# Reordering the expert block of a fused attention, expert and mixing kernel: first products evacuated and next tokens turned ahead of the split of the next expert's first weights

## The chip, the cores and the metric

One core of a Trainium2 chip runs the whole program. The metric is the device time of one execution in microseconds (us), the median of several executions; lower is better. Engines are named as in the profile: PE (matrix products and transposes), PEld (its weight loads), DVE (VectorE), ACT (ScalarE), POOL (GpSimd), SP (which issues most DMAs).

## What is computed

The reference is windowed attention over 4 batches of 576 tokens, then a layer of 8 experts that picks one expert for each token, then a gated mixing over the sequence. The change lies in the middle layer:

```python
for s in range(S):
    fresh_e = int(np.argmax(logits[b, s]))
    if s == 0 or local_gate[b, s] < 0.5:
        e = fresh_e
    else:
        e = prev_e if prev_e >= 0 else fresh_e
    prev_e = e
    ...
    h = np.maximum(x[b, s] @ w1[e], 0.0)
    out[b, s] = p[e] * (h @ w2[e])
```

A token has 512 values, an expert has w1 (512 x 1024) and w2 (1024 x 512), all float32.

## The kernel before

**Blocks.** Tokens are sorted into blocks of 128 rows that share an expert. At most 25 blocks exist; 23 (0 to 22) hold tokens in these runs, and the last ones stand inside branches. Which tokens a block has, which expert, and whether the expert differs from that of the block before, is computed on the chip (the routing) in three lists: blocks 0 and 1, blocks 2 to 5, blocks 6 to 24. The routing of the last batch still runs during blocks 0 to 2: its steps wait in a list `stages`, and `pop` puts some of them between the products (after the second quarter of stage 1 and after parts 2 and 6 of stage 2).

**Precision.** A float32 factor is used as the sum of a high part (a rounded copy, made by ACT) and a low part (the difference, by DVE or POOL). A product is then three matmuls: high x high (L999), low weights x high tokens (L1000), high weights x low tokens (L1001).

**One block.** `block(j)` (L1157) does stage 1 of block j+1 (`stage1`, 24 matmuls in four quarters kk, into the PSUM tile `hp`) and stage 2 of block j (`stage2`, 24 matmuls L1033 to L1035 in eight parts f, into `yp`), and around them:

- `gather` (L967): DVE copies an index column (L970), POOL issues the indirect DMA (L972) that brings the rows of a block into `xs`. It is called at the block's start for block j+3; the later calls with j+3 find it done.
- `fetch` (L564): SP issues four DMAs for a block's w1 into `raw1` or w2 into `raw2`, which move data only if the expert changes. Each has to wait until the pieces of the raw tile have been read.
- `divide` (L950): the split of the next weights, inside a branch (L958) that is taken if the expert changes. Four pieces c: ACT copies raw to the high part (L549), then DVE (c = 0, 2, 3) or POOL (c = 1) subtracts (L550). `divide(1, j+2)` makes `w1h` and `w1l`, `divide(2, j+1)` makes `w2h` and `w2l`. It is taken ten times for each. A piece of `w1h` can be overwritten once the quarter of stage 1 that reads it is done.
- `bend` (L1003): ACT takes the ReLU of the two halves of `hp` to `h` (L1006). It needs the end of stage 1.
- `turn_x` (L974): PE transposes the gathered rows of block j+2 to `xTp` (L976), ACT copies the high part `xh` (L984), DVE subtracts the low part `xl` (L985).
- `turn_h` (L1009): PE transposes `h` (L1012); in two halves ACT copies `hh` (L1022) and DVE subtracts `hl` (L1023), the second `hh` after the first `hl`. Stage 2 of the next block reads them.
- `narrow` (L1055): a piece of the mixing's float64 weights is turned to float32, in blocks 5 to 16: five DVE operations and one on ACT (L1065 to L1071), split one block later on ACT and POOL (tiles `wih`, `wil`, `woh`, `wol`).
- `place` (L478), the last routing step, comes in block 2 after part 2 of stage 2: DVE copies `bc` (L482), POOL multiplies (L486), DVE reduces and combines (L487 to L496).

**Order.** The order on each engine is the order of the calls, written by hand (`manual_schedule`); an engine runs its instructions in that order, and a waiting instruction holds those behind it. In `block(j)` it is, with the values that matter here: stage 1 of j+1, split of w1 for j+2, ReLU of j+1, turning of the tokens of j+2, stage 2 of j, split of w2 for j+1, store of j, turning of h of j+1.

Of the kernel before, what the change touches and what calls it, by code (L numbers as in the profile page):

```python
# [69 lines left out]
def moe_stack(ctx: ExitStack, tc: tile.TileContext, q, k, v, w_gate, w_local, w1, w2, w_in, w_sp, b_sp, w_out, out):  # L70
# [9 lines left out]

    # ---------------------------------------------------------------- constants
    warm = const.tile([128, 512], BF16, name="warm")
# [38 lines left out]

    # ---------------------------------------------------------------- routing state
    idxacc = rt.tile([128, NCOL], F32, name="idxacc")
    slot_i = rt.tile([128, LB], I32, name="slot_i")
    sel_all = rt.tile([128, LB, E], F32, name="sel_all")
    # of each token: its block among its expert's blocks, its row in it, and its weight
    trips = rt.tile([128, LB, 3], F32, name="trips")
# [7 lines left out]
    def steps(f):  # L135
        """A closure's parts, between which other work may come."""
        g = f()
        if g is not None:
            yield from g
# [9 lines left out]
    def router(b, xT, pieces, sides, bank):  # L149
        """Adds the closures that route batch b to stages."""  # L150
        st = {}
# [93 lines left out]
        def scan3():  # L245
            sv = st["sv"]
            if b == 0:
                # How many blocks of each expert hold tokens of the first batch.
                ci = rt2.tile([E, 2], I32, name="ci")
                nc.vector.tensor_scalar(out=ci[:, 0:1], in0=state["cum"], scalar1=127.0, scalar2=None, op0=ALU.add)  # L250
                nc.vector.tensor_scalar(out=ci[:, 1:2], in0=ci[:, 0:1], scalar1=7, scalar2=None, op0=ALU.arith_shift_right)
                state["first"] = rt.tile([E, 1], F32, name="first")
                nc.vector.tensor_copy(state["first"], ci[:, 1:2])
            nc.scalar.activation(sv[:, S:640], sv[:, 512:S].bitcast(F32), AF.Copy)
# [134 lines left out]
        def rows():  # L389
# [18 lines left out]
            if b < 3:  # L408
                return
            # The block before which every row of the first batch is there, if there is such a one.  # L410
            it = iota128[0:1, 0:n]
# [17 lines left out]
        def after():  # L429
            """Where this list's blocks of each expert begin, how many they are, and where the next list begins."""  # L430
            sf, en, nb, (j0, j1) = st["sf"], st["en"], st["nb"], LISTS[b]
            D = state["D"]
            base = rt2.tile([E, 1], F32, name="base")
            if b == 1:
                nc.vector.tensor_copy(base, sf)
            else:
                nc.vector.tensor_scalar(out=base, in0=sf, scalar1=state["got"], scalar2=float(j0), op0=ALU.subtract, op1=ALU.add)
            nc.vector.tensor_scalar(out=D[:, 2 * b - 2], in0=ident[0:E, 0:E], scalar1=base, scalar2=None, op0=ALU.mult)
            yield
            if b == 3:  # L440
                return
            n = j1 - j0
            tk = rt2.tile([E, 1], F32, name="tk")
            nc.vector.tensor_scalar(out=tk, in0=sf, scalar1=-1.0, scalar2=float(n), op0=ALU.mult, op1=ALU.add)
            yield
            nc.vector.tensor_scalar(out=tk, in0=tk, scalar1=0.0, scalar2=nb, op0=ALU.max, op1=ALU.min)
            yield
            got = rt.tile([E, 1], F32, name=f"got{b}")
            if b == 1:
                nc.vector.tensor_copy(got, tk)  # L450
            else:
                nc.vector.tensor_add(got, state["got"], tk)
            nc.vector.tensor_scalar(out=D[:, 2 * b - 1], in0=ident[0:E, 0:E], scalar1=got, scalar2=None, op0=ALU.mult)
            yield
            last = rt2.tile([E, 1], F32, name="last")
            nc.vector.tensor_scalar(out=last, in0=sf, scalar1=float(n), scalar2=None, op0=ALU.is_lt)
            yield
            l2 = rt2.tile([E, 1], F32, name="l2")
            nc.vector.tensor_scalar(out=l2, in0=en, scalar1=float(n), scalar2=None, op0=ALU.is_ge)
            yield  # L460
            nc.vector.tensor_mul(last, last, l2)
            yield
            st["last"], st["new"] = last, got
# [75 lines left out]
    stages = []  # L539
    state["bank"] = R()  # L540

    # ---------------------------------------------------------------- attention
    sc = ctx.enter_context(tc.tile_pool(name="sc", bufs=1))
# [11 lines left out]
    def fetch1(j, i):  # L555
        """The first two blocks have their own copies of w1, the first one also of w2, and use them as they are."""
        e = value(1, j, [ET.SP], E - 1)
        nc.sync.dma_start(first1[j][:, i:i + 1], w1[ds(e, 1), 128 * i:128 * i + 128].rearrange("o (k p) f -> p (o k) f", p=128))
# [23 lines left out]
    def attention(aw, ap, qkp, plan):  # L582
# [13 lines left out]
        npair = B * 4  # L596
        # A head's keys fill half of the rows and meet zeros in the other half, which lets the products use both heads' queries as they lie.
        kz = [[aw.tile([128, S], F32, name=f"kz{p}{hh}", bufs=1) for hh in range(2)] for p in range(2)]
# [4 lines left out]
        def load_qk(u):  # L603
            b, pr = divmod(u, 4)
            n, c = (96, 6) if pr < 2 else (72, 8)
            for w_, src in ((0, q), (1, k)):
                t = qkp.tile([96, 1024], F32, name=f"qk{w_}", bufs=3)
                if w_:
                    # Keys come head by head, each partition's tokens in one piece.
                    tv = t[0:n, 0:2 * c * D].rearrange("p (h m) -> p h m", h=2)  # L610
# [52 lines left out]
        def T_k(u, hh, tag="T"):  # L663
            """Turns a head's keys two neighbours at a time, whose dimensions then lie in the two halves of the rows."""
            def f():
# [157 lines left out]
        fill = deque()  # L823
# [14 lines left out]
        def feed(i):  # L838
            """Parts of the routing, as many as a step can take along; the tensor engine gets one only when its operands had time to be made."""
            nonlocal budget  # L840
# [83 lines left out]

    # ---------------------------------------------------------------- experts
    aps, aws, qks, w1s, mws, mps, xps = [ExitStack() for _ in range(7)]
# [34 lines left out]
    def own(key, pool, shape, dt, tag=None):  # L961
        """A tile that stays for all blocks."""
        if key not in P:
# [91 lines left out]
    def narrow(c):  # L1055
        """A piece of the float64 weights as float32, and that in two parts."""
        if c < 8:
# [16 lines left out]
    def early(kind, c=0):  # L1074
        """The steps of blocks 0 and 1 that run beside the last of the attention."""
        def bankT():
# [22 lines left out]
    def pop(kind="any"):  # L1099
        """The next step of the routing; "pe": if the tensor engine has a part in it; "rest": all up to such a one."""  # L1100
        while stages and (kind == "any" or (kind == "pe") == hasattr(stages[0], "on_pe")):
# [4 lines left out]
    def ahead(what, j, must=False):  # L1106
        """Issues the gathers or fetches up to block j that the lists already give."""
        while done[what] <= min(j, NBLK - 1):
# [35 lines left out]
    def gate(j, engines=None):  # L1144
        """Blocks that every count of tokens fills run straight, the others where they hold any."""
        if j < SURE:
# [10 lines left out]
    def block(j):  # L1157
# [4 lines left out]
        if nxt:  # L1162
            with gate(j + 1, [ET.PE]):
                for kk in range(4):
                    stage1(j + 1, hp, [kk])
                    if kk in POP1:
                        pop("pe")
                        pop("rest")
        if nxt2:
            ahead(1, j + 2, must=True)  # L1170
            divide(1, j + 2, j == 0)
        if nxt:
            bend(j + 1, hp)
        ahead(1, j + 3)
        if nxt2:
            ahead("gather", j + 2, must=True)
            turn_x(j + 2, bank_x())
        ahead("gather", j + 3)
        yp = bank_y()
        for f in range(8):  # L1180
# [46 lines left out]

    # ---------------------------------------------------------------- gated mixing over the sequence
    gr = ctx.enter_context(tc.tile_pool(name="gr", bufs=1, side="right", reuse_waits="tile"))
# [11 lines left out]
    def mixing(gw):  # L1241
# [17 lines left out]
        def turn_w(si):  # L1259
            """A part of the weights over the sequence, turned; the last 64 columns twice, for the two places of a batch's last tokens."""  # L1260
            w2x = G["w2x"]
# [61 lines left out]
        def norm3(g):  # L1323
            vr, _ = vn[g]
            if g % 9 == 4:
                # The last 64 tokens of two batches: a batch's high parts and, in the other half, its low parts.
                for t, a, z in ((tails[0], slice(0, 64), slice(64, 128)), (tails[1], slice(64, 128), slice(0, 64))):
# [59 lines left out]
        def project(b, gh, gl):  # L1387
# [3 lines left out]
            for ah, al, i in items:  # L1391
                o = gw.tile([128, C], F32, name="o", bufs=2)
                # The very last piece in two halves, so that less of it is left at the end.
                for cs in [slice(0, C)] if (b, i) != (B - 1, 3) else [slice(0, 256), slice(256, C)]:
# [86 lines left out]
```

## Time and profile before

| | us |
|---|---|
| median of 3 runs | 706.55 |
| lowest and highest run | 706.11, 706.99 |
| span of the profiled execution, first to last instruction | 705.2 |
| median run less that span (before the first and after the last instruction) | 1.35 |
| PE busy in the span | 672.2 (95%) |
| DVE, ACT, POOL busy | 423.9, 386.0, 194.2 |

The page gives no time of its own for the profiled execution beside its span, so the span and the 1.35 us around it are set against the median. The clock that the throttle granted PE is at 90% or more of full speed in all 40 slices. In rows of a timeline the columns are: start and duration in us, engine, source line, operation, output and inputs, count, and in brackets the idle time of the engine just before and what ended it. A merged row (x3) runs from the first start to the last end. A line with "DVEq" or "ACTq" names that engine's instruction sequencer, here at the branch of `divide`.

### The profile page before, as it was taken

Reading aid. Unit: us, or ns where it says so; the run is one execution under the profiler, and the core shown is the slowest. Engines: PE = TensorE matmul, PEld = TensorE weight load, DVE = VectorE, ACT = ScalarE, POOL = GpSimd, SP = SyncE. Lnnn points to the kernel's source line nnn. Section 1 sums busy time; section 2 is a strip of 40 time slices with the busy share of each in tenths; the row PEclk is TensorE's granted clock in tenths of the full one; section 3 lists DMA queues with packets and bytes.
Section 4 is the critical chain, followed back from the end, with each engine's and each line's share of the span. In section 5 each row is a group of like instructions: output and inputs, shape, how many; then the busy total and the mean of one; then the engine's idle time right before and its main releaser. Section 6 shows DMA issues by size and latency. Waiting matters only on the chain. (4 is left out here: it accounts for less than half of the span.)

```text
span 705.2 us, 14287 instructions
## 1 busy us (share of the span) xinstructions
PE 672.2 (95%) x4395; PEld 571.1 (81%) x4396; DVE 423.9 (60%) x1379; ACT 386.0 (55%) x780; POOL 194.2 (28%) x226
## 2 busy tenths in 40 slices
PE   8999898989999999999999999897999999999998
PEld 6989797885478788787788877775898998998997
DVE  4667869777966747877866656342664164154151
ACT  5788777653635646666665556333735336335322
POOL 6443434341424405425424254112010110000000
PEclk9999999999999999999999999999999999999999
DMA  6776545594446776586556746415110220200102
GB/s 152 180 174 152 129 118 131 189 347 126 138 150 204 249 283 231 199 314 213 192 195 223 283 142 233 165 32 162 30 46 0 76 60 1 75 16 1 60 2 74
DMA packets 90644, 101.36 MB, mean 144 GB/s; under 512 B 49984, under 2 KB 60992, under 8 KB 90560
## 3 DMA queue, kind: packets, MB, share of 16 engines
q1 hardware_dynamic: 87120, 89.10, 39.7%
q0 software_dynamic: 3440, 11.27, 5.0%
q8 instruction: 36, 0.59, 0.3%
q14 instruction: 48, 0.39, 0.2%
HBM read 139.68 MB, written 17.30 MB: 223 GB/s over the span
## 5 line engine op out<-in xcount | busy, mean ns | idle before, releaser
L1001 PE MATMUL hp<-w1h,xl 128*128 128x512 f32 x168 | 66.9, 398 | 7.0 <-DVEq L958 6.1
L1033 PE MATMUL yp<-w2h,hh 128*128 128x512 f32 x176 | 71.6, 407 | 0.2 <-ACT hh L1022 0.2
L1035 PE MATMUL yp<-w2h,hl 128*128 128x512 f32 x176 | 69.9, 397 | 1.7 <-DVE hl L1023 1.7
L972 POOL DMA_INDIRECT xs<-x_d,ix x25 | 30.8, 1232 | 144.7 <-PE xTp L976 56.1
L1034 PE MATMUL yp<-w2l,hh 128*128 128x512 f32 x176 | 69.6, 395 | 0.0
L743 POOL TENSOR_TENSOR ms<-ms,mxa 96x384 f32<-96x384 f32 (+2 forms) x64 | 51.1, 799 | 64.9 <-DVE mxa L740 39.7
L999 PE MATMUL hp<-w1h,xh 128*128 128x512 f32 x168 | 68.4, 407 | 0.2 <-issue 0.2
L1000 PE MATMUL hp<-w1l,xh 128*128 128x512 f32 x168 | 66.4, 395 | 0.0
L740 DVE CUSTOM_DVE_ANT_0 ms<-S,masks 96x128 f32<-96x128 f32 (+2 forms) x224 | 54.4, 249 | 16.8 <-PE S L729 8.2
L550 DVE TENSOR_TENSOR w2l<-raw,w2h 128x1024 fp32r<-128x1024 f32 x30 | 48.7, 1649 | 24.5 <-ACT w2h L549 24.2
L550 DVE TENSOR_TENSOR w1l<-raw,w1h 128x1024 fp32r<-128x1024 f32 x30 | 55.7, 1902 | 5.3 <-ACT w1h L549 4.6
L729 PE MATMUL S<-kz,qT 128*96 128x128 f32 (+2 forms) x448 | 53.2, 259 | 0.4 <-POOL vt L632 0.4
L1151 POOL DMA_INDIRECT yg<-y_d,slot_i x14 | 13.4, 958 | 138.5 <-PE tr L1283 102.6
L776 PE MATMUL PV<-vt,ptS 128*96 128x65 f32 (+2 forms) x448 | 44.4, 240 | 7.0 <-issue 2.9
L1023 DVE TENSOR_TENSOR hl<-hTp,hh 128x512 fp32r<-128x512 f32 x44 | 30.3, 689 | 33.9 <-ACT hh L1022 31.9
L1022 ACT ACTIVATE hh<-hTp 128x512 fp32r<-128x512 f32 x44 | 26.2, 596 | 43.6 <-DVE hl L1023 38.2
L776 PEld LDWEIGHTS PV<-vt,ptS 128*96 128x96 f32 (+2 forms) x448 | 38.7, 156 | 9.7 <-issue 3.6
L729 PEld LDWEIGHTS S<-kz,qT 128*72 128x72 f32 (+1 forms) x448 | 45.4, 155 | 1.2 <-POOL vt L626 0.9
L1001 PEld LDWEIGHTS hp<-w1h,xl 128*128 128x128 f32 x168 | 31.5, 188 | 17.1 <-DVEq L958 8.4
L549 ACT ACTIVATE w2h<-raw 128x1024 fp32r<-128x1024 f32 x40 | 41.1, 1060 | 6.0 <-PE yp L1035 3.4
L549 ACT ACTIVATE gtiles<-gt 128x288 fp32r<-128x288 f32 (+2 forms) x48 | 15.7, 359 | 48.0 <-DVE gt L1377 48.0
L1035 PEld LDWEIGHTS yp<-w2h,hl 128*128 128x128 f32 x176 | 33.1, 188 | 10.7 <-DVE hl L1023 3.0
(309 smaller groups left out, 1825.5 us busy)
## 6 DMA issues: line engine op xcount, KB each, us to landing
raw<-in_moe_w SPq DMA_DIRECT2D x188, 512.0 KB
y_d<-y SPq DMA_DIRECT2D x30, 256.0 KB
qk<-in_q SPq DMA_DIRECT2D x32, 144.0 KB
qk<-in_k SPq DMA_DIRECT2D x32, 144.0 KB
x_d<-xo SPq DMA_DIRECT2D x32, 144.0 KB
scratch<-in_moe_w_in SPq DMA_DIRECT2D x8, 512.0 KB
out<-o SPq DMA_DIRECT2D x15, 256.0 KB
vt<-in_v SPq DMA_DIRECT2D x48, 64.0 KB
```

Source lines behind the costliest of these rows:

```text
L549: nc.scalar.activation(dst_h, src, AF.Copy)
L550: (eng or nc.vector).tensor_tensor(out=dst_l, in0=src, in1=dst_h.bitcast(F32), op=ALU.subtract)
L729: nc.tensor.matmul(ps[0:nq, j, 0:nk], l, r, start=True, stop=True)
L740: nc.vector.tensor_tensor_reduce(out=ms[0:nq, j, 0:nk], in0=ps[0:nq, j, 0:nk], in1=masks[0:nq, m, 0:nk], scale=-0.125, scalar=3.0e38, op0= ...
L743: nc.gpsimd.tensor_tensor(out=ms[0:nq, 0:nb, 0:nk], in0=ms[0:nq, 0:nb, 0:nk], in1=mx[0:nq, 0:nb].unsqueeze(2).to_broadcast([nq, nb, nk]), ...
L776: nc.tensor.matmul(ops[0:nq, j], ptS[0:nk, j, 0:nq], r, start=True, stop=True)
L999: nc.tensor.matmul(ps[n], xh[:, kk], wh[:, kk, cs], start=(kk == 0), stop=False)
L1000: nc.tensor.matmul(ps[n], xh[:, kk], wl[:, kk, cs], start=False, stop=False)
L1001: nc.tensor.matmul(ps[n], xl[:, kk], wh[:, kk, cs], start=False, stop=(kk == 3))
L1033: nc.tensor.matmul(ps, hh[:, f], P["w2h"][:, f], start=(f == 0), stop=False)
L1034: nc.tensor.matmul(ps, hh[:, f], P["w2l"][:, f], start=False, stop=False)
L1035: nc.tensor.matmul(ps, hl[:, f], P["w2h"][:, f], start=False, stop=(f == 7))
```

## The change

The split of the next w1 and the fetch behind it move from between stage 1 and the ReLU to behind the turning of the next tokens. Nothing else differs but comments, which are gone.

```diff
@@ def block(j)
-        if nxt2:
-            ahead(1, j + 2, must=True)
-            divide(1, j + 2, j == 0)
         if nxt:
             bend(j + 1, hp)
-        ahead(1, j + 3)
         if nxt2:
             ahead("gather", j + 2, must=True)
             turn_x(j + 2, bank_x())
         ahead("gather", j + 3)
+        if nxt2:
+            ahead(1, j + 2, must=True)
+            divide(1, j + 2, j == 0)
+        ahead(1, j + 3)
         yp = bank_y()
```

## Rows read from the trace of the kernel before

**Rows 1.** Stretches of one block: length, PE, PEld, DVE, ACT, POOL, clock, DMA, GB/s.
```profile
309.90:322.40 12.50, 12.50 (x62) 10.21 (x61) 11.27 (x13) 9.27 (x14) 4.59 (x4) 1.00 0.64 237
296.10:309.90 13.80, 12.80 (x62) 10.18 (x61) 8.89 (x13) 7.65 (x12) 6.59 (x5) 1.00 0.70 243
440.30:455.20 14.90, 12.74 (x59) 10.12 (x60) 5.06 (x7) 3.43 (x7) 0.97 (x2) 1.00 0.49 177
232.40:246.00 13.60, 12.70 (x62) 10.09 (x61) 9.99 (x10) 8.11 (x12) 5.78 (x3) 1.00 0.63 215
```

**Rows 2.** Waits of PE in the expert blocks: total, times, longest.
```profile
PE hp L1001 <- DVEq L958: 6.1, 5, 2.2
```

**Rows 3.** Timeline, block 12 and the start of block 13: w1 split taken.
```profile
341.79 3.91 ACT L549 ACTIVATE w1h<-raw 128x1024 fp32r<-128x1024 f32 x4
341.91 0.60 PE L976 MATMUL xTp<-ident,xs 128*128 128x128 f32 x4
344.06 5.71 DVE L550 TENSOR_TENSOR w1l<-raw,w1h 128x1024 fp32r<-128x1024 f32 x3 [0.42 <-ACT w1h L549]
344.38 1.74 POOL L972 DMA_INDIRECT xs<-x_d,ix  x1 [7.88 <-PE yp L1035]
345.60 1.06 ACT L1006 ACTIVATE h<-hp 128x512 f32<-128x512 f32 x2
346.34 3.43 DVE L550 TENSOR_TENSOR w1l<-raw,w1h 128x1024 fp32r<-128x1024 f32 x1
349.05 0.40 PE L1000 MATMUL hp<-w1l,xh 128*128 128x512 f32 x1
349.70 0.68 DVE L985 TENSOR_TENSOR xl<-xTp,xh 128x512 fp32r<-128x512 f32 x1
```

**Rows 4.** Timeline, block 11, where the w1 split is not taken.
```profile
329.39 0.60 PE L976 MATMUL xTp<-ident,xs 128*128 128x128 f32 x4
329.65 1.09 ACT L1006 ACTIVATE h<-hp 128x512 f32<-128x512 f32 x2 [2.26 <-PE hp L1001]
330.62 0.60 ACT L984 ACTIVATE xh<-xTp 128x512 fp32r<-128x512 f32 x1
331.26 0.69 DVE L985 TENSOR_TENSOR xl<-xTp,xh 128x512 fp32r<-128x512 f32 x1 [2.01 <-ACT xh L984]
331.82 1.30 POOL L550 TENSOR_TENSOR wil<-scratch,wih 128x512 fp32r<-128x512 f32 x1 [0.87 <-ACT wih L549]
```

**Rows 5.** Timeline, block 2 and the start of block 3.
```profile
212.18 2.40 POOL L550 TENSOR_TENSOR w1l<-raw,w1h 128x1024 fp32r<-128x1024 f32 x1
212.52 4.28 DVE L550 TENSOR_TENSOR w1l<-raw,w1h 128x1024 fp32r<-128x1024 f32 x2 [0.51 <-ACT w1h L549]
212.57 0.60 PE L976 MATMUL xTp<-ident,xs 128*128 128x128 f32 x4
217.32 0.18 DVE L482 COPY bc<-R 128x40 f32<-128x40 f32 x1
223.94 0.69 DVE L1023 TENSOR_TENSOR hl<-hTp,hh 128x512 fp32r<-128x512 f32 x1 [0.94 <-DVEq L958]
226.30 0.40 PE L1034 MATMUL yp<-w2l,hh 128*128 128x512 f32 x1
226.53 0.40 PE L1035 MATMUL yp<-w2h,hl 128*128 128x512 f32 x1
```

**Rows 6.** Timeline, end of block 3 and block 4: both splits follow each other.
```profile
232.74 2.93 POOL L550 TENSOR_TENSOR w2l<-raw,w2h 128x1024 fp32r<-128x1024 f32 x1 [1.55 <-ACT w2h L549]
233.95 5.08 DVE L550 TENSOR_TENSOR w2l<-raw,w2h 128x1024 fp32r<-128x1024 f32 x3
240.21 0.40 PE L1035 MATMUL yp<-w2h,hl 128*128 128x512 f32 x1
```

**Rows 7.** Timeline, blocks 0 and 1: the list work on DVE and the product behind it.
```profile
194.41 0.17 DVE L386 TENSOR_TENSOR lz<-la,lz 8x19 f32<-8x19 f32 x1
195.18 0.35 PE L394 MATMUL R<-lz,onesE 8*1 8x19 f32 x8
```

## The prediction

> **What bounds the kernel now.** The summary of engines comes first: PE is busy in nearly all of the span, so only the gaps of PE can be won. The table of stretches shows where they are in the expert blocks: a clean block takes 12.50 us, all of it PE busy, and some blocks take more [rows 1]. The list of PE's waits names the place: five times PE stood before L1001, the product with the low part of the tokens, 6.1 us in all, released by DVE behind the branch of the split [rows 2]. The timeline of such a place gives the reason. In block 12 the three DVE pieces of the w1 split run from 344.06 to 349.77, and only then comes `xl`, which is short; `xl` ends at 350.38, while stage 1 of block 14 is under way and wants it 0.23 us after 349.05 [rows 3]. So the split of weights that are wanted later holds up tokens that are wanted first. ACT has the same order: `h` starts at 345.60, behind the four copies [rows 3], where without a split it starts 0.26 us after the first transpose [rows 4].
>
> A wait costs more than its idle time, since PE's pipeline fills again. The stretch 296.10 to 309.90 takes 13.80 us, 1.3 more than a clean block; there are four of that kind (13.8, 13.8, 13.7, 13.7), together 5.0 us. The stretch after block 19 takes 14.9, 2.4 more; the one at 232.40, 13.6, 1.1 more [rows 1].
>
> **The change, part by part.** Nothing is added or removed; ACT, DVE, POOL, SP get the same instructions in another order, and PE's own order stays.
>
> Tokens ahead of the split, regular blocks. Where no split stands in front, `h` starts 0.26 us after the first transpose, `xh` 0.97 after `h`, `xl` 1.61 after `h` [rows 4]. In block 12 the first transpose is at 341.91 [rows 3], which gives `h` at 342.2, `xh` 343.1 to 343.7, `xl` 343.8 to 344.5: 5.9 us sooner than now and 4.8 before it is wanted. The wait goes: 5.0 and 2.4 us, **7.4 in all**, if nothing else is late.
>
> What can be late is the split. Its ACT copies start now at 341.79 and take 3.91 us [rows 3]; they move behind `xh`, to 343.7, and are done at 344.8, 345.75, 346.7 and 347.65. POOL's gather, 344.38 plus about a microsecond (its 1.74 less its own wait beside DVE's piece [rows 3], an estimate), is in front of DVE's piece 0, so that it runs 345.3 to 346.55 (1.2 us each when alone: 4.28 less the 2.06 us for which POOL's piece still ran gives 2.2 for two [rows 5]). POOL's piece 1 follows to 348.95 (2.40 us [rows 5]), piece 2 to 350.15, and piece 3 to 351.3, or to 352.6 if POOL's conversion of 1.30 us [rows 4] gets in between. Stage 1 wants the low parts of quarters 1, 2 and 3 at 349.05 plus 6, 12 and 18 products of 0.23 us (the pace of neighbours in [rows 5]): 350.4, 351.8, 353.2. All are in time, the last by 0.6 to 1.9 us. This is the cover of the edit: if it is gone, each microsecond costs one in each of nine splits (block 0's has routing around it).
>
> The rows show that DVE and POOL don't work side by side on these pieces: a DVE piece that meets a POOL piece lasts 3.43 us instead of 1.2 [rows 3], and two DVE pieces end 2.2 us after POOL's [rows 5]. I reckon with that. The Trainium skill, page "SBUF — State Buffer", section "SBUF: two separate sides", says that VectorE and GpSimd share a port pair under an exclusive lock, held for the whole instruction; it speaks against the change, which pushes the split towards POOL's other work. By it the sum is the one below; were the two only to share, it would be that of the first rival.
>
> Block 2, the routing behind the split. After the split in block 2 DVE has the last routing step, then `hl` for stage 2 of block 3, and there is little slack: `hl` ends at 224.63 and is wanted at 226.53 [rows 5]. Now the copies start early, during stage 1, as each quarter sets its weights free. In the new order they wait: first transpose 212.57 [rows 5], `xh` 213.8 to 214.4, copies done at 215.5, 216.5, 217.4, 218.4. DVE's piece 0 ends at 216.8, POOL's piece 1 at 219.2, DVE's other two 2.2 later, at 221.4, so `bc` starts at 221.3 instead of 217.32 [rows 5], 4.0 later. Everything to `hl` moves along: `hl` ends at 228.6, **PE waits 2.1 us** at 226.53.
>
> Blocks 3 and 4. The second half of `hh` comes at 228.7, so `h` only at 229.4, `xh` ends at 231.0, the w1 copies for block 5 are done between 232.05 and 234.85, DVE's piece 0 at 233.3, POOL's at 235.7, the rest at 237.9. Stage 1 of block 5 gets them in time, and its 1.1 us of wait for `xl` goes. But the w2 split follows on the same engines. Its POOL piece has its copy at 236.9 and stands at the port until 237.9, then runs to 240.3. Now DVE's three w2 pieces end 3.36 us after POOL's (239.03 against 235.67 [rows 6]), which puts them at 243.7 and `hl` at 244.4. Stage 2 of block 4 wants it at 240.21, less 1.1, plus 2.1: 241.2. **PE waits 3.2 us.** If DVE keeps the port from w1's last piece to w2's three, it is 1.3 (`hl` at 242.1, then 0.4 for POOL's late piece). I take 3.2, as POOL's piece has stood there longest, and as POOL went first in the same place now [rows 6]. So the two blocks cost 2.1 + 3.2 - 1.1 = 4.2, at the other end 2.3; were the delay in block 2 covered, -1.1.
>
> Block 0. The list work for the last list also moves behind the split; it ends at 194.58 and PE takes its result at 195.18 [rows 7]. `xl` no longer stands between (0.68), POOL's piece, now later, does: 0.7 later, 0.2 us of wait (0 to 0.6).
>
> Fetches. SP's order stays. The w1 fetch waits for the pieces read, up to 2 us later, for weights that are split a block or more afterwards; I cost it at nothing, under cover of that block of 12.5 us.
>
> Sum: -7.4 + 4.2 + 0.2 = -3.0 us on the span of 705.2, so 702.2; with the 1.35 us around it, and the median being as much above the span, 706.55 - 3.0 = **703.5**. With the DVE-first end 701.6.
>
> **The rivals.** *All of it is won.* If block 2's split is done in time (the copies come sooner, or the two engines overlap better than the rows say), neither new wait appears, the 1.1 goes too: 706.55 - 8.5 = 698.1. Against it: 4.0 us of delay meets 1.9 of slack. Chance 0.15.
>
> *The start eats it up.* The w2 fetch for block 4 is issued only when DVE has passed its branch behind the routing step, which is 4.0 us later too. If its data then hold up the w2 split by another 2 us, stage 2 of block 4 waits those as well: 705.5, within the bound of no change. For it: the w2 copies, planned at 234.85, move about as much as the fetch, so there is no new slack. Chance 0.13.
>
> *Slower.* The split's last piece is late in every block with a conversion. Its place is quarter 3 of stage 1 in the block after each w1 split; it decides from 0.6 us. If the copies start 1.5 us later than I put them, 0.9 us is lost in each of six such blocks, 5.4 in all: 708.9. For it: the copies now stand behind `h` and `xh`, which wait for PE, where before they ran ahead of the end of stage 1. Against it: ACT is busy 9.3 of 12.5 us in a block with a split [rows 1], and `h` and `xh` start promptly wherever no split is in front [rows 4]. Chance 0.12.
>
> *It does not do what it says*: `xl` would still be late for another reason. But it starts the moment the last piece ends, 4.1 us after `h` began, where 1.6 are enough without a split [rows 3, 4]. Within the slower case.
>
> **How the numbers follow.** Forecast with its DVE-first variant 0.60, the three rivals 0.15, 0.13, 0.12. A measurement of this kernel tells about 0.2% (1.4 us) from no change, so faster means under 705.1. The forecast lies there, mostly (0.58 of 0.60), and the first rival: 0.73. Same, 705.1 to 708.0: the second rival and 0.02: 0.15. Slower: 0.12. The range runs from the first rival, 698.0, through both ends of the early cost to 706.0, over the second; outside it are the slower case and the edges of the others, about 0.2.
>
> **What would show it.** Right: PE's wait at L1001 behind the branch gone from blocks 9 to 20, those blocks at 12.5 us, `xl` right behind `xh`, `h` right behind stage 1; PE waiting at L1035 for `hl` near 226.5 for about 2 us and near 241 for 1 to 3; `bc` starting near 221. Wrong: L1000 waiting for `w1l` after a split, or block 3 starting stage 2 without a wait.

## The result: slower by 0.6%

The changed kernel takes 711.35 us (median of 20 runs), the kernel before on the same chip 707.1; the ratio is 1.0057 [1.0037, 1.0077], or 4.0 us. Forecast were 703.5 us and a range from 698.0 to 706.0. The profiled executions, on which the rest goes, have spans of 709.3 and 705.2.

**The waits for `xl` are gone.** The list of PE's waits in the expert blocks of the changed kernel (total, times, longest) answers to [rows 2]; its first two lines are:

```profile
PE hp L1000 <- DVE w1l L550: 2.6, 4, 0.7
PE hp L1000 <- POOL w1l L550: 2.6, 3, 1.2
```

No line with L1001 is left. In its place stand waits at L1000: now it is the low part of the weights that is late. The stretches from one turning of tokens to the next (columns as in [rows 1]):

```profile
267.87:280.38 12.51, 12.51 (x61) 10.27 (x60) 9.05 (x10) 7.98 (x12) 5.69 (x3) 1.00 0.25 82
318.84:333.74 14.90, 13.04 (x61) 10.09 (x60) 12.62 (x14) 8.76 (x13) 5.52 (x3) 1.00 0.42 159
```

Block 6, the first of the two, is clean. The one of block 10 is 2.4 us longer than a clean block; those that start at 292.88, 346.26 and 411.26 are 0.9, 2.4 and 1.5 longer. Together 7.2 us are lost at L1000 where 7.4 were won at L1001. The rest of the loss is at the start: stages 2 of blocks 3 and 4 last 7.81 and 9.87 instead of 5.85 and 5.84, stage 1 of block 5 lasts 5.85 instead of 7.01: +1.96 + 4.03 - 1.16 = 4.8 us. Block 0 adds 0.7: stage 1 of block 2 lasts 7.07 instead of 6.33. Together that is 5.3 us more, 5.6 + 7.1 - 7.4; the spans differ by 4.1 only, as this execution was 2.05 us ahead when stage 1 of block 2 began (190.15 against 192.20). That start differs from profile to profile (190.7 to 195.0 in those with the old order in the first blocks), so it is not put down to the change.

Where block 10's 2.4 us come from, in its timeline; compare [rows 3] (the same place in the old order) and [rows 4]:

```profile
318.64 0.68 DVE L1023 TENSOR_TENSOR hl<-hTp,hh 128x512 fp32r<-128x512 f32 x1
318.84 0.60 PE L976 MATMUL xTp<-ident,xs 128*128 128x128 f32 x4
319.36 0.60 ACT L1022 ACTIVATE hh<-hTp 128x512 fp32r<-128x512 f32 x1 [0.92 <-DVE hl L1023]
321.05 0.72 ACT L1066 ACTIVATE scratch<-scratch,expo_bias 128x512 int32<-128x512 int32 x1 [1.09 <-DVE scratch L1065]
321.68 1.07 ACT L1006 ACTIVATE h<-hp 128x512 f32<-128x512 f32 x2
323.11 3.91 ACT L549 ACTIVATE w1h<-raw 128x1024 fp32r<-128x1024 f32 x4
323.55 0.68 DVE L985 TENSOR_TENSOR xl<-xTp,xh 128x512 fp32r<-128x512 f32 x1
324.21 1.23 DVE L550 TENSOR_TENSOR w1l<-raw,w1h 128x1024 fp32r<-128x1024 f32 x1
324.38 1.90 POOL L972 DMA_INDIRECT xs<-x_d,ix  x1 [8.14 <-DVE xl L985]
326.10 6.04 DVE L550 TENSOR_TENSOR w1l<-raw,w1h 128x1024 fp32r<-128x1024 f32 x2 [0.67 <-ACT w1h L549]
326.30 2.39 POOL L550 TENSOR_TENSOR w1l<-raw,w1h 128x1024 fp32r<-128x1024 f32 x1
328.64 1.28 POOL L550 TENSOR_TENSOR wil<-scratch,wih 128x512 fp32r<-128x512 f32 x1
328.74 0.50 PE L1000 MATMUL hp<-w1l,xh 128*128 128x512 f32 x1 [1.19 <-POOL w1l L550]
331.06 0.50 PE L1000 MATMUL hp<-w1l,xh 128*128 128x512 f32 x1 [0.67 <-DVE w1l L550]
332.29 0.69 DVE L1023 TENSOR_TENSOR hl<-hTp,hh 128x512 fp32r<-128x512 f32 x1
333.01 0.60 ACT L1022 ACTIVATE hh<-hTp 128x512 fp32r<-128x512 f32 x1 [4.23 <-DVE hl L1023]
334.71 0.73 ACT L1066 ACTIVATE scratch<-scratch,expo_bias 128x512 int32<-128x512 int32 x1 [1.09 <-DVE scratch L1065]
335.34 1.06 ACT L1006 ACTIVATE h<-hp 128x512 f32<-128x512 f32 x2
```

Read it from PE back. L1000 waits for quarters 1 and 2 of `w1l`. POOL's piece starts at 326.30, behind a gather that took 1.90 beside a DVE piece, and POOL's conversion follows it at once; DVE's next piece, begun at 326.10, gets through only behind both, and DVE's two end at 332.14, 2.2 after POOL's 329.92. All of it starts late: the copies begin 4.27 after the first transpose, where the forecast had 1.8 (343.7 against 341.91), because `h` stands on ACT behind the second `hh` and L1066, and these wait for DVE. DVE's own queue is as late: `xl` starts at 323.55, behind the conversion's last step on DVE (L1071, to 323.41), not behind `xh` (to 323.23). And it goes round: DVE's late pieces make `hl` late (332.29), this the second `hh` (333.01), this L1066 and the next `h` (335.34). In block 6, where `h` waits only for PE, the same chain starts on time: the copies are 1.7 after the transpose, as forecast, and no quarter is late:

```profile
268.13 1.09 ACT L1006 ACTIVATE h<-hp 128x512 f32<-128x512 f32 x2 [1.89 <-PE hp L1001]
269.58 3.91 ACT L549 ACTIVATE w1h<-raw 128x1024 fp32r<-128x1024 f32 x4
271.68 2.51 POOL L550 TENSOR_TENSOR w1l<-raw,w1h 128x1024 fp32r<-128x1024 f32 x1 [1.49 <-ACT w1h L549]
272.58 4.93 DVE L550 TENSOR_TENSOR w1l<-raw,w1h 128x1024 fp32r<-128x1024 f32 x2 [0.67 <-ACT w1h L549]
274.14 2.28 POOL L550 TENSOR_TENSOR wil<-scratch,wih 128x512 fp32r<-128x512 f32 x1
```

ACT waits for data too, as the list of waits of 285 to 432 shows (before: 0.9 us, 3 times, in the same stretch); whether this link matters is the first question of the second group of runs:

```profile
ACT w2h L549 <- DMA raw<-in_moe_w: 14.3, 16, 1.8
```

The start, in the timeline of blocks 2 and 3, beside [rows 5]:

```profile
219.73 0.18 DVE L482 COPY bc<-R 128x40 f32<-128x40 f32 x1
226.32 0.49 PE L1034 MATMUL yp<-w2l,hh 128*128 128x512 f32 x1 [1.16 <-DVEq L958]
226.35 0.69 DVE L1023 TENSOR_TENSOR hl<-hTp,hh 128x512 fp32r<-128x512 f32 x1 [0.95 <-DVEq L958]
```

`bc` starts 8.46 after the first transpose (211.27), before 4.75 (212.57 to 217.32): 3.7 later, forecast 4.0. In block 0 PE waits for the list work (before, this product waited for nothing):

```profile
194.02 0.20 PE L394 MATMUL R<-lz,onesE 8*1 8x19 f32 x2 [0.39 <-DVE lz L386]
```

### The profile page after: what moved, and what is told of

Same layout as the page of the kernel before. It is cut to its first block, busy times and chain, and to the rows that moved or that the text cites. A ratio compares the mean times of both kernels' runs of the same rounds, so it can differ in the third digit from the quotient of the medians.

```text
span 709.3 us, 14278 instructions
## 1 busy us (share of the span) xinstructions
PE 674.1 (95%) x4395; PEld 572.1 (81%) x4396; DVE 429.4 (61%) x1379; ACT 384.6 (54%) x780; POOL 188.1 (27%) x226
## 5 line engine op out<-in xcount | busy, mean ns | idle before, releaser
L1000 PE MATMUL hp<-w1l,xh 128*128 128x512 f32 x168 | 67.2, 400 | 5.3 <-DVE w1l L550 2.6
L972 POOL DMA_INDIRECT xs<-x_d,ix x25 | 28.1, 1125 | 154.6 <-DVEq L958 46.4
L1001 PE MATMUL hp<-w1h,xl 128*128 128x512 f32 x168 | 66.4, 395 | 0.0
L550 DVE TENSOR_TENSOR w1l<-raw,w1h 128x1024 fp32r<-128x1024 f32 x30 | 60.0, 2027 | 7.5 <-ACT w1h L549 7.0
L1000 PEld LDWEIGHTS hp<-w1l,xh 128*128 128x128 f32 x168 | 31.7, 189 | 14.7 <-DVE w1l L550 4.4
```

What stands on the lines that cost most here:

```text
L550: (eng or nc.vector).tensor_tensor(out=dst_l, in0=src, in1=dst_h.bitcast(F32), op=ALU.subtract)
L1000: nc.tensor.matmul(ps[n], xh[:, kk], wl[:, kk, cs], start=False, stop=False)
L1001: nc.tensor.matmul(ps[n], xl[:, kk], wh[:, kk, cs], start=False, stop=(kk == 3))
```

## The experiments

The ratios are to the kernel before on the same chip. "Excess" is what the stages 1 behind a w1 split last over 5.85 us each; in the changed kernel it is 7.1. Each excess is that of one profiled execution. In three profiles with the changed order behind block 3 and nothing else moved there it is 7.1, 6.8 and 7.1, but in two profiles of one kernel, the last below, it is 0.1 and 2.4, so differences of under 2 us between such sums are weak. In the expectations, Theory A is: two losses, one at the start and one that arises anew in the regular blocks; Theory B: one loss at the start, whose delay is what is seen later.

**The new order from block 4 on, and up to block 3.**

In the cuts of code, shortened, `split1` and `tokens` are the two groups of calls that the change swapped, each put into a function; `...` stands for lines left out.

```diff
+        if j < 4:      # second kernel: if j >= 4
+            split1()
         if nxt:
             bend(j + 1, hp)
-        if nxt2:
-            ahead("gather", j + 2, must=True)
-            turn_x(j + 2, bank_x())
...
+        tokens()
+        if not (j < 4):
+            split1()
```

> New order in blocks 4 to 22 only, old order in blocks 0 to 3. Theory A (two separate losses: at the start the last routing step and the w2 split stand behind the late w1 split, +4.9 us by block 5; later the waits for xl go, but a loop takes their place: late split, so late w2 fetch, so late w2 copies, so late second hh and conversion on ACT, so late h, so late split): the start is as before, the later blocks as in the changed kernel, +0.4 us in sum; ratio to before 0.999 to 1.002, PE still waiting at L1000 after the splits of blocks 8, 10, 12 and 17, 6.9 us in all with refilling. Theory B (the start delays everything downstream, its DMAs too, and the later waits are an echo of that): with the start undone the waits at L1000 are gone and the ratio is 0.989 to 0.992.

> New order in blocks 0 to 3 only, old order from block 4 on. Theory A: the start costs what it costs in the changed kernel, 4.9 us by block 5, and the five waits for xl from block 9 on are all there again: ratio 1.006 to 1.008. Theory B: the same start, and its echo in later blocks: more than 1.008, with waits beyond the old ones.

From block 4 on: 0.9984 [0.9967, 1.0002], just under the range of Theory A. Stages 2 of blocks 3 and 4 are clean, the excess is there all the same (0.85, 2.26, 2.30, 1.40). Up to block 3: 1.0086 [1.0061, 1.0111], with the waits of the start (stages 2 of 7.84 and 8.34) and all old waits at L1001 but block 5's; stage 1 of block 21 is 1.5 longer than before (9.79 against 8.27). This run does not decide between the theories, as its interval lies on both sides of 1.008. The two, -1.1 and +6.1 us, add up to 5.0, within the interval of the whole. The run from block 4 on decides: with the start undone, the waits at L1000 are all there, so they are no echo of it.

**The old order in block 2 alone.**

```diff
+        if j == 2:
+            split1()
...
+        tokens()
+        if j != 2:
+            split1()
```

> Changed kernel with the old order in block 2 alone. Forecast's reading (the routing step behind the split of block 2 is late, and block 4's wait follows from it): stage 2 of block 3 is clean (5.85) and stage 2 of block 4 waits for hl 1 us or less; steady blocks as in the changed kernel, with the excess of 7.1; so the ratio falls from 1.006 by about 0.006 to 1.000 (0.998 to 1.002). Rival (block 3's new order makes the wait in stage 2 of block 4 by itself): stage 2 of block 4 still lasts over 8 us, the ratio is 1.003 or more.

1.0003 [0.9978, 1.0029]. Stage 2 of block 3 is clean (5.85); stage 2 of block 4 lasts 7.31, waiting 1.21 for `hl`, a little more than expected. So some 1.5 us of block 4's loss come from the new order in block 3 itself, where the prediction had put it down to block 2 whole. The rest follows from block 2's delay: 2.6 of the 4.0 us of the profiled execution, 1.0 of the 2.5 that six other profiles with the same start show.

**Without the conversion's exponent (L1066), changed order and old.** Left out: the exponent of the mixing's converted weights.

```diff
-        nc.scalar.activation(sc, sc, AF.Relu, bias=P["bias"], scale=2.0 ** 23)
```

> The changed kernel without the one ACT operation of the float64 conversion (the exponent step), so that ACT no longer waits for DVE in front of h; part of the mixing weights' computation is left out. Theory A (the loop closes through this ACT operation, which waits for DVE behind the second hl): the loop is cut, h starts within 0.2 us of the end of stage 1 in every block, the split 1.5 us later, the waits at L1000 go, about 6.9 us less than the changed kernel: ratio to before 0.994 to 0.998, with the 4.9 us of the start still there. Rival C (the port: the split is late because POOL's subtraction and conversion hold up DVE's pieces): the waits at L1000 stay, ratio 1.003 to 1.007.

> Control for the run without the exponent operation: the kernel before without it (part of the mixing weights' computation is left out). Theory A: in the old order nothing that PE waits for stands behind it, the waits at L1001 stay as they are: ratio 0.998 to 1.002. If the operation itself costs time in any order: under 0.997, and the gain of the earlier run without it says nothing of a loop.

Changed order: 0.9962 [0.994, 0.9984], the stages 1 at 5.87, 5.89, 6.18 and 6.00; the start's waits stay. Old order: 0.9993 [0.9966, 1.0021], waits at L1001 as ever. ACT's wait for data, 11.1 us in the first, is not much smaller than in the changed kernel (14.3), and yet the waits are nearly gone.

**The w2 fetch ahead of the w1 fetch** in blocks 6, 8, 10, 12, 15, 17, 19.

```diff
         ahead("gather", j + 3)
+        if j in (6, 8, 10, 12, 15, 17, 19):
+            ahead(2, j + 2)
         if nxt2:
...
-            if j:
+            if j and j not in (6, 8, 10, 12, 15, 17, 19):
                 divide(2, j + 1)
```

(In these blocks the w2 branch is not taken, so it is left out.)

> The changed kernel, but in the blocks whose w1 split is taken (6, 8, 10, 12, 15, 17, 19) SP issues the w2 fetch ahead of the w1 fetch, and the w2 branch, which these runs don't take there, is left out, so that this fetch no longer waits for the w1 split. Theory A (the loop runs through the late w2 fetch): the ACT waits for w2 data, 14.3 us in the later blocks of the changed kernel, fall under 3 us, h is prompt again, the waits at L1000 nearly vanish; the start still costs 4.9 us; ratio 0.993 to 0.998. Rival D (the loop needs no DMA: ACT and DVE are late by the order alone): the waits at L1000 stay and the ratio is 1.002 to 1.007.

1.0014 [0.9989, 1.0038], between what Theory A and its rival had. ACT's wait for data is gone, but the stages 1 still last 6.74, 7.89, 7.90 and 6.63, an excess of 5.8. Its timeline in block 10 shows the loop without a transfer in it:

```profile
318.39 0.60 ACT L1022 ACTIVATE hh<-hTp 128x512 fp32r<-128x512 f32 x1 [3.98 <-DVE hl L1023]
320.08 0.72 ACT L1066 ACTIVATE scratch<-scratch,expo_bias 128x512 int32<-128x512 int32 x1 [1.10 <-DVE scratch L1065]
322.14 3.91 ACT L549 ACTIVATE w1h<-raw 128x1024 fp32r<-128x1024 f32 x4
331.82 0.60 ACT L1022 ACTIVATE hh<-hTp 128x512 fp32r<-128x512 f32 x1 [4.27 <-DVE hl L1023]
```

So the loop does not need the w2 fetch, and that part of Theory A falls.

**Three other orders of the same work**: ReLU, split, tokens; then tokens, split, ReLU; then pieces 0 to 2 of the split, tokens, piece 3, ReLU. The lines are the orders that result, shortened.

```python
         if nxt:                    # first
             bend(j + 1, hp)
         if nxt2:
             ahead(1, j + 2, must=True)
             divide(1, j + 2, j == 0)
         ahead(1, j + 3)
         if nxt2:
             turn_x(j + 2, bank_x())
...
         if nxt2:                   # second
             turn_x(j + 2, bank_x())
             divide(1, j + 2, j == 0)
         if nxt:
             bend(j + 1, hp)
...
         if nxt2:                   # third
             divide(1, j + 2, j == 0, (0, 1, 2))
             turn_x(j + 2, bank_x())
             divide(1, j + 2, j == 0, (3,))
         if nxt:
             bend(j + 1, hp)
```

> Half of the change: the ReLU ahead of the split, the tokens behind it as in the old order. Theory A: the split now waits for the end of stage 1 (copies about 1 us after it instead of before it), so the routing at the start is late as in the changed kernel, and xl stays behind the split: the old waits at L1001 are there and longer by about 1 us each: ratio 1.008 to 1.016. Rival E (the harm comes from the tokens' copy and subtraction standing ahead): 0.998 to 1.003.

> The other half: the tokens ahead of the split, the ReLU behind it. Theory A: the split still waits for the end of stage 1, but starts 1 us sooner than in the changed kernel; the waits at L1001 go, the start costs 3 to 4 us instead of 4.9, the loop is weaker, the waits at L1000 under 4 us; ratio 0.996 to 1.002. Rival E: as bad as the changed kernel, 1.004 to 1.008.

> A third order: the split's pieces 0 to 2, then the turning of the tokens, then piece 3, then the ReLU; piece 3 needs the end of stage 1 anyway, so xl gets ahead of it at no cost and the split starts as early as in the old order. Theory A: neither the start nor the later fetches are delayed, xl is in time everywhere: all 8.5 us of waits at L1001 go, ratio 0.987 to 0.990. If instead any order with xl ahead of a piece of the split brings the waits at L1000, or the second branch costs as much as it saves: 0.997 or more.

ReLU first: 1.0368 [1.0341, 1.0395], more than twice the upper end of what was expected. The split stands behind `h` as in the changed kernel, and `xl` behind the split as in the old one (PE's waits from 285 to 432):

```profile
PE hp L1001 <- DVEq L958: 12.8, 4, 3.5
```

Tokens first and ReLU last: 0.996 [0.9936, 0.9984], no excess, the start's waits still there. Tokens between the pieces: 0.9921 [0.9895, 0.9947], between the two outcomes that were expected, span 698.2, with few waits left (stage 2 of block 4 lasts 6.81, stage 1 of block 21 6.67). So the tokens ahead of the split do win; the ReLU ahead of it takes it back. With the ReLU last, the second `hh` and L1066 still stand in front of the copies on ACT, but not the ReLU: in block 10 the copies start 1.81 after the first transpose instead of 4.27, where the ReLU itself takes 1.07, so the delay that comes round is smaller too.

**Tokens first, ReLU last, from block 4 on.**

```diff
+        if j < 4:
+            split1()
-        if nxt:
+        if nxt and j < 4:
             bend(j + 1, hp)
...
+        tokens()
+        if not (j < 4):
+            split1()
+            if nxt:
+                bend(j + 1, hp)
```

> Tokens, split, ReLU in blocks 4 and later, the old order in blocks 0 to 3. Both losses are left out and the waits for xl too, so the two effects add: ratio 0.996 less the start's 0.007 = 0.989 (0.986 to 0.992), all stages 1 and 2 at 5.85 but that of block 5 with its old 1.1. If the start's loss only moved later blocks back in time (an echo), it is 0.994 or more.

0.9933 [0.9903, 0.9964], between the range expected and the 0.994 of the rival; all stages 1 behind block 5 are clean. One new wait of 1.79, PE's turning of `h` behind the late ReLU, takes a part of what is missing.

**Which link closes the loop?** First L1066 and the two DVE steps behind it, moved behind the tokens.

```diff
-        nc.scalar.activation(sc, sc, AF.Relu, bias=P["bias"], scale=2.0 ** 23)
...
-        return lambda: split(hi_, lo_, mf, nc.gpsimd)
+        def later():   # L1066, L1070, L1071, then rest.append(split)
...
         turn_x(j + 2, bank_x())
+        if expo:
+            expo.pop()()
```

> Theory: in the changed kernel h is late because ACT has L1066 in front of it, which waits for DVE (L1065 behind both hl). With the same work, but L1066 and the two DVE steps behind it put behind the turning of the next tokens, h starts at the end of the second hh: about 1.7 us sooner in the late blocks (320.0 instead of 321.68 in block 10), and the w1 copies, now behind L1066, about 0.8 us sooner. The waits at L1000, together 7.1 us of excess in four stretches of stage 1, should then fall to 1 to 4 us, the ratio from 1.006 to 0.998 to 1.002. The starting blocks keep their two waits. Rival (DVE's queue as a whole is the loop, whatever stands in front of h on ACT): excess of 6 us or more stays and the ratio is 1.004 or more. If no wait at all is left: about 0.996, as without the operation.

1.0685 [1.0639, 1.0731], and it tells nothing of the theory: the words of the next piece but one are now fetched into the buffer before the moved step reads it, so that DVE waits for that transfer, ten times (the line shows six of them, four more are for `in_moe_w_out`), and the converted weights get the signs of another piece:

```profile
DVE scratch L1072 <- DMA scratch<-in_moe_w_in: 32.8, 6, 9.7
```

With the call that fetches the words moved behind the step as well:

```diff
         if expo:
             expo.pop()()
+        if 0 <= j + 1 - NARROW0 < 12:
+            words(j + 1 - NARROW0)
```

> As in the run with L1066 behind the tokens, but the fetch of the next words for the conversion is called behind it too, so that DVE's step with the sign bits waits for no transfer. Theory (L1066 in front of h is a link of the loop): with the same work in the program, h starts 1.7 us sooner in the late blocks and the w1 copies 0.8 us sooner; the excess in stage 1 falls from 7.1 to 1 to 4 us, the ratio from 1.006 to 0.998 to 1.002. Rival (DVE's queue is the loop whatever stands in front of h on ACT): excess of 6 us or more, ratio 1.004 or more.

1.0084 [1.0053, 1.0116], an excess of 10.9 in three stages 1: a miss. The timeline of block 8 shows why:

```profile
295.70 1.08 ACT L1006 ACTIVATE h<-hp 128x512 f32<-128x512 f32 x2
298.97 0.68 DVE L1072 SCALAR_TENSOR_TENSOR scratch<-scratch 128x512 int32<-128x512 int32 x1
299.69 0.69 DVE L1073 SCALAR_TENSOR_TENSOR scratch<-scratch 128x512 f32<-128x512 f32 x1
300.30 7.18 DVE L550 TENSOR_TENSOR w1l<-raw,w1h 128x1024 fp32r<-128x1024 f32 x3
```

`h` now stands right behind the second `hh`, which ends at 295.81, but the two DVE steps have come in between `xl` and the split. The edit moved two things at once, so two runs moved one each: the sign step L1070 taken from DVE (left out: the signs of the mixing weights), and L1066 given to DVE.

```diff
-        nc.vector.scalar_tensor_tensor(out=sc, in0=high, scalar=-2 ** 31, in1=sc, ...)   # first kernel
...
-        nc.scalar.activation(sc, sc, AF.Relu, bias=P["bias"], scale=2.0 ** 23)            # second kernel
+        nc.vector.tensor_scalar(out=sc, in0=sc, scalar1=2.0 ** 23, scalar2=-896.0 * 2.0 ** 23, op0=ALU.mult, op1=ALU.add)
```

> Changed kernel without L1070, one DVE step of 0.69 us in each conversion (left out: the signs of the mixing weights). L1066 still stands in front of the ReLU on ACT, while DVE reaches the tokens' low part and the split 0.7 us sooner. Theory (L1066 on ACT is the link): the excess of 7.1 us in stage 1 mostly stays, 5 us or more, ratio 1.003 or more. Rival (DVE's queue between the second hl and the split is the link, and a bit of relief there does as much as taking L1066 away): excess 0 to 2.5, ratio 0.996 to 0.999.

> Changed kernel with the exponent's step (L1066) on DVE instead of ACT, the same result: the ReLU stands right behind the second hh, 1.0 to 1.7 us sooner in the late blocks, and DVE's queue in front of the split is 0.4 us longer. Theory (L1066 on ACT is the link): excess falls from 7.1 to 0 to 3 us, ratio 0.996 to 1.000, as without the operation. Rival (DVE's queue is the link): excess stays at 7 or grows, ratio 1.005 to 1.010.

Without the sign step: 0.9999 [0.9973, 1.0025], and an excess of 1.2. With L1066 on DVE: 0.9999 [0.998, 1.0017], and an excess of 3.9; the waits behind DVE's `w1l` are gone, those behind POOL's stay:

```profile
PE hp L1000 <- POOL w1l L550: 2.8, 4, 1.1
```

Neither theory is right alone. By the excess, 0.7 us less on DVE takes 6 of the 7 us away although L1066 still stands in front of `h`; L1066 away from ACT takes 3 although DVE has 0.4 more to do. The medians don't tell the two apart: both are 0.9999.

The traces show what each did. With L1066 on DVE, `h` starts 0.26 after the first transpose in block 10 (318.43) and the copies 1.70, just as forecast; but `xl` stands behind DVE's steps, 3.95 after it, so the split's first piece and POOL's are late all the same, and 0.75 is lost:

```profile
320.13 3.91 ACT L549 ACTIVATE w1h<-raw 128x1024 fp32r<-128x1024 f32 x4
322.38 0.68 DVE L985 TENSOR_TENSOR xl<-xTp,xh 128x512 fp32r<-128x512 f32 x1
325.04 2.52 POOL L550 TENSOR_TENSOR w1l<-raw,w1h 128x1024 fp32r<-128x1024 f32 x1
```

Without the sign step the copies are still late, 3.31 after the transpose in block 10 and 3.36 in block 17. In block 17 that is as late as in the changed kernel, and DVE's pieces start at the same places too, but only 0.06 is lost instead of 1.48. POOL's gather begins 0.5 sooner, ahead of DVE's first piece and not behind its start, and takes half the time, so that POOL's piece starts 2.1 after the copies instead of 3.2. Block 17 without the sign step, copies from 410.77:

```profile
411.51 0.96 POOL L972 DMA_INDIRECT xs<-x_d,ix  x1 [8.23 <-DVE ix L970]
411.87 1.23 DVE L550 TENSOR_TENSOR w1l<-raw,w1h 128x1024 fp32r<-128x1024 f32 x1 [0.26 <-ACT w1h L549]
412.86 2.48 POOL L550 TENSOR_TENSOR w1l<-raw,w1h 128x1024 fp32r<-128x1024 f32 x1 [0.39 <-ACT w1h L549]
```

In the changed kernel, copies from 414.62:

```profile
415.71 1.23 DVE L550 TENSOR_TENSOR w1l<-raw,w1h 128x1024 fp32r<-128x1024 f32 x1
415.88 1.89 POOL L972 DMA_INDIRECT xs<-x_d,ix  x1 [8.07 <-PE yp L1034]
417.80 2.40 POOL L550 TENSOR_TENSOR w1l<-raw,w1h 128x1024 fp32r<-128x1024 f32 x1
```

So the split's low parts hang on three things: ACT's copies, DVE's queue in front of the first piece, and whether the gather gets ahead of that piece. Some tenths on any of them decide.

**POOL's conversion given to DVE.**

```diff
-        return lambda: split(hi_, lo_, mf, nc.gpsimd)
+        return lambda: split(hi_, lo_, mf)
```

> Changed kernel with the conversion's low part (1.28 us on POOL) given to DVE, where it comes behind the split's pieces. Theory (POOL's two operations back to back keep DVE's third piece waiting): the third piece ends 1.3 us sooner, so the second wait in a stretch (0.66 behind DVE's w1l) goes, the first (1.2, behind POOL's w1l) stays; hl comes about 0.6 us sooner, so h and the split too, by as much again in the next round. Excess in stage 1 falls from 7.1 to 3 to 5 us, the ratio from 1.006 to 0.999 to 1.003. Rival (DVE's pieces are late by their copies on ACT, or POOL's conversion does not hold DVE up): the waits behind DVE's w1l stay at 0.6 or grow by the 0.7 that DVE gets to do, ratio 1.005 to 1.009.

0.9998 [0.9972, 1.0024]. The excess falls from 7.1 to 1.65, more than expected: one wait is left, 1.65 us in stage 1 of block 14, behind copies that start 4.47 after the first transpose of block 12. In block 10 the delay that comes round is smaller: `h` starts 1.42 after the first transpose (321.07) instead of 2.84, the copies 2.85 instead of 4.27. And the same delay costs less: in block 8 of the changed kernel, where the copies start 2.81 after the transpose, 0.9 us are lost, here 0.06. Block 10:

```profile
322.49 1.07 ACT L1006 ACTIVATE h<-hp 128x512 f32<-128x512 f32 x2
323.92 3.91 ACT L549 ACTIVATE w1h<-raw 128x1024 fp32r<-128x1024 f32 x4
326.91 4.83 DVE L550 TENSOR_TENSOR w1l<-raw,w1h 128x1024 fp32r<-128x1024 f32 x2 [0.67 <-ACT w1h L549]
327.11 2.41 POOL L550 TENSOR_TENSOR w1l<-raw,w1h 128x1024 fp32r<-128x1024 f32 x1
```

The two DVE pieces take 4.83 instead of 6.04 (block 10 of the changed kernel): 1.2 less, the time of the POOL operation that no longer comes between. Then the same with the old order in blocks 0 to 3, the control (the old order everywhere), and the first of these once more beside it:

> The changed order from block 4 on, with the conversion's low part on DVE: the start's waits and all but one of the steady waits are left out. If the two losses add, the ratio is that with the conversion on DVE, 1.000, less the start's 0.0065: 0.9935 (0.991 to 0.996), so the change's own order wins about what was forecast for regular blocks (7.4 us of 706 is 0.0105, less 1.65 for the one wait left and 1.1 at block 4 that stays). If the start only shifts the waits, 0.997 or more.

> Control: the kernel before (old order everywhere) with the conversion's low part on DVE. If POOL's conversion matters only to the new order, the waits at L1001 stay (6 to 7 us of idle time) and the ratio is 0.998 to 1.002, so that what the new order gains with the conversion on DVE is the order's. Rival (the conversion on POOL also holds up the old order's split, whose last piece keeps the tokens' low part waiting): the waits at L1001 fall by about 0.6 each and the ratio is 0.993 to 0.996.

> The changed order from block 4 on with the conversion's low part on DVE once more, beside the control on the same chip: if the order wins what was forecast for regular blocks, 0.992 (0.989 to 0.995), at least 0.004 below the control.

0.9921 [0.9892, 0.9949] and, beside the control, 0.9897 [0.9836, 0.9957]; the control 1.0 [0.9975, 1.0024]. The control keeps its old waits; in the profile of the first (span 697.1) no stage 1 behind block 5 lasts over 5.93, in that of the second two do, by 0.9 and 1.5. PE's waits in the expert blocks, of the control:

```profile
PE hp L1001 <- DVE xl L985: 3.9, 4, 1.0
PE hp L1001 <- DVEq L958: 2.2, 1, 2.2
```

So the conversion's move alone is worth nothing, the order alone (from block 4 on) 1.1 us, and the two together 5.6 and 7.3, with intervals (3.6 to 7.6, 3.0 to 11.6) that hold the forecast's 7.4: the order wins about that, once the split has its cover.

## Why the prediction was wrong

**Right: what bounds, and that it goes.** All five waits at L1001 in the regular blocks vanish, `xl` comes before it is wanted, and most of the 7.4 us are there to be won: the three kernels that have the tokens ahead of the split's last piece and lose little or nothing at the start (tokens between the pieces, tokens first from block 4 on, and the one just above) gain 4.7 to 7.3.

**Right in size: the start.** Forecast 2.1 + 3.2 - 1.1 + 0.2 = 4.4; measured 1.96 + 4.03 - 1.16 + 0.74 = 5.6 in the profiled run. Block 4's share varies (2.5 in six other profiles with the same start, 4.0 in two), which makes it 4.0 to 5.6; a part of that share, some 1.5 us, is block 3's own. Block 0 was put too low, 0.2 (at most 0.6) against 0.7.

**The step that failed** is the cover of the split: "Their copies ... move behind `xh`, to 343.7". It took the prompt `h` of a block without a split [rows 4] for the new order too. But in front of `h` on ACT stand the second `hh` and L1066, both waiting for DVE, and DVE is late there because of the split one block before, which is itself late. DVE's queue holds up `xl` and the first piece as well: that piece starts 3.91 and 5.37 after the first transpose in blocks 8 and 10, where the forecast had 3.4 (345.3). The copies start 1.0 us later than forecast in block 8 and 2.5 later in block 10 (2.81 and 4.27 after the first transpose, against 1.8). PE's waits are 0.6 and 1.9 us, and the blocks lose 0.9 and 2.4, each wait costing some tenths more than its idle time. Block 6, 0.1 early, loses nothing. That the forecast's slack of 0.6 fits these waits (0.4 and 1.9 are over it) is in part luck: it was the slack of the last piece, and the late ones are quarters 1 and 2. POOL's conversion goes ahead of DVE's piece 2, not behind it, and the gather takes 1.9 beside DVE's first piece, where the forecast had about a microsecond ahead of it. So the lengths of the pieces, the port and the due times held, and the start they were counted from did not: the delay of the split was followed for one block only, and the loop closes over two.

**The slower rival came true**, nearly as priced: 0.9 us in each of six blocks for copies 1.5 late, 708.9; it was 7.2 in four blocks, and it took away just what was won. "ACT is busy 9.3 of 12.5 us" was no argument against it, since ACT stood and waited for DVE (at `hh` for `hl` 25.3 us from 285 to 432, before 15.4).

**The port.** The prediction went by the rule that DVE and POOL exclude each other for a whole operation. The trace bears it out: DVE's two pieces end 2.2 us behind POOL's last in block 10, about the time of two pieces (1.23 alone), and they take 1.2 less when POOL's conversion is away. The Trainium skill, page "SBUF — State Buffer", section "SBUF: two separate sides", says the same of the lock: whoever starts first has the pair for the whole instruction.

**Fetches at nothing** was a small error: the data do come late (14.3 us of ACT's waits), but taking that away gives back only 1.3 us of excess, and 0.4% by ratios whose intervals just touch.

**What stays open.** How much of the loop belongs to ACT, how much to DVE and how much to the gather can't be said in microseconds: the two edits that moved one step each take 6 and 3 of the 7 us, so they don't add, and each excess is of one profile. No run moved the gather alone. And why POOL's conversion goes ahead of DVE's waiting piece in block 10, but behind it in block 6, was not tried.

## What to carry to other kernels

When a step is moved behind others on an in-order engine, count its new start from what really stands in front of it there, and follow the delay that it causes round to the same place one period later: if it comes back, tenths of slack are no cover. An order that frees the first consumer is worth trying in variants that keep the second one's cover (here the late piece of the split alone behind the tokens, 0.9921, or the low-priority conversion moved to another engine). And test a new order in two halves of the run: two losses and a gain that cancel look like one small loss.

## What was not expected of the hardware

- Who goes next at the port is not first come, first served for the profile's times: in block 10 DVE's piece is begun at 326.10, POOL's two at 326.30 and 328.64, and both of POOL's are done by 329.92, ahead of it; in block 6 POOL's conversion is begun at 274.14 and takes 2.28 instead of 1.28; by that length a piece of DVE's goes first.
- From block 4 on, the gather's issue on POOL takes 1.87 to 1.90 us where a DVE piece of the split has begun before it and 0.94 to 0.96 where none has, even when it begins during `xl` or a piece begins during it. In blocks 8, 10, 12 and 17 it held up POOL's piece of the split by about a microsecond.
